# Six small edits to a convolution and spectral-mixing kernel: yeT's order, the conv band's set-up, the first load on two queues, halved last stores, Y's transposes behind the mixing's, and 15 junk matmuls

## Chip, cores, metric

One core of one Trainium2 chip. The metric is the device time of one execution in microseconds (us), the median of repeated runs. The time of the kernel before was 181.24 us (three runs, 180.69 to 181.25). Each execution also reports the span of the core's program, 1.8 us less than the time in the median, up to 3.1 us less in single executions; the profile's clock starts with the span. A transfer "lands" when its completion is signalled, here some 0.3 us after its last packet (177.89 against 177.55 us for the last store of the kernel before).

## The reference

Two layers in a row, cut to what matters:

```python
# x: (8, 3264, 192) float32; weight: (8 heads, 7 taps)
w = softmax(weight, axis=-1)
x[b, s, h, :] = sum_k w[h, k] * x_padded[b, s + k, h, :]     # causal conv, one filter per head
X = rfft(x, axis=1)[:, :64]                                   # 64 lowest modes
Y[b, m, :] = X[b, m, :] @ (w_r[m] + 1j * w_i[m])              # 64 complex 192 x 192 mixes
u = x + irfft(Y, n=3264)
out = u + relu(u @ w_ch)
```

## The kernel before

The program has three stages. Until about 66 us x is loaded by GpSimd (float32 cast to bf16 on the way), convolved by matmuls with a banded matrix, and brought to 64 modes. Until about 108 us the modes are mixed: 16 groups of weights, each loaded in two halves behind x on the same GpSimd queue. From there to the end the result is built in 108 units of two batches by one window of 122 positions, and stored.

The parts that the change touches (cuts marked):

```python
# start: softmax weights and one unit of x come by other queues than GpSimd's
nc.scalar.dma_start(out=wraw, in_=weight)                    # 224 bytes
nc.sync.dma_start(out=x32[:], in_=...)                       # 768 KB, x of batch 0, windows 10 to 17
load_unit(0, 2)                                              # first load of the GpSimd stream, 432 KB
...
# conv band: masks from an iota, then softmax, then 7 scaled masks summed by matmuls
nc.vector.tensor_copy(out=diagc[...], in_=diag[...])         # waits for GpSimd's iota
... softmax of wraw on VectorE and ScalarE ...
for k in range(KK):
    nc.vector.scalar_tensor_tensor(out=scaled[:, k, :, :], ...)
    for o in bps:                                            # the same sum into two banks
        nc.tensor.matmul(o[:, 0:H * NB], ident[:], scaled[:, k, :, :], ...)
for g in range(4):                                           # 4 copies: ScalarE takes bank 0, VectorE bank 1
    ...

# mixing: two groups g make 128 rows of Y (ymix), transposed into yeT
def mix_t(g, ymix):
    for t in range(2):
        nc.tensor.transpose(et[:, t, :], ymix[:, 64 * t:64 * t + P], ident[:])
    nc.vector.tensor_copy(out=yeT[:, :, P * (g // 2):P * (g // 2) + P], in_=et)

# 12 of the 16 groups go back from yeT to zy, two times 8 transposes
def y_back(half):
    for i in range(4):
        for e in range(2):
            nc.tensor.transpose(tp[...], yeT[:, e, 4 * half + i:n * B:B], ident[:])   # stride of 8
    nc.vector.tensor_copy(out=zy[...], in_=tp[...])

# the products with w_ch, first thing of the last stage
nc.tensor.matmul(o, yeT[:, e, b:2 * MODES * B:B], wn[:, :], ...)                      # stride of 8

for g in range(NGRP):
    m = mix(g)                                               # 12 matmuls, waits for the group's weights
    ... transposes of x (tp) that fill TensorE between the groups ...
        if g in (12, 13):
            y_back(g - 12)
    if m is not None:
        mix_t(g, m)
    ...

# last stage: one store per window and half of the batches, 384 KB, issued by SP
def finish_unit(u, zp):
    nc.vector.tensor_tensor(out=t[...], in0=zp[...], in1=x_all[...], op=ALU.add)
    if k == 0:
        return
    nc.sync.dma_start(out=dst, in_=t[r0:r1, :, :])
```

Of the kernel before, what the change touches and what calls it, by code (L numbers as in the profile page):

```python
# [9 lines left out]
ALU = mybir.AluOpType  # L10
ACT = mybir.ActivationFunctionType
AX = mybir.AxisListType
F32 = mybir.dt.float32
BF16 = mybir.dt.bfloat16
# [4 lines left out]
def kernel(  # L19
# [9 lines left out]
    nc = tc.nc  # L29
    B, S, D = x.shape  # L30
    H, KK = weight.shape
    MODES = moe_w_r.shape[0]
# [3 lines left out]
    P = 128  # L36
    WIN = 122
    OV = KK - 1
# [13 lines left out]
    constp = ctx.enter_context(tc.tile_pool(name="const", bufs=1))  # L52
# [20 lines left out]
    def load_last():  # L73
# [8 lines left out]
    ident = constp.tile([P, P], BF16, tag="ident")  # L82
# [10 lines left out]
    cband = cp1.tile([P, H, P], BF16, tag="cband")  # L93
# [3 lines left out]
    sp = setup_stack.enter_context(tc.tile_pool(name="setup", bufs=1))  # L97
    wraw = sp.tile([1, H, KK], F32, tag="wraw")
    nc.scalar.dma_start(out=wraw[:].rearrange("p h k -> p (h k)"),
                        in_=bass.AP(tensor=weight.tensor, offset=weight.offset, ap=[[H * KK, 1], [1, H * KK]]))  # L100

    x32 = sp.tile([P, 8, D], F32, tag="x32")
    nc.sync.dma_start(out=x32[:], in_=bass.AP(tensor=x.tensor, offset=x.offset + (WIN * 10 - OV) * D,
                                              ap=[[D, P], [WIN * D, 8], [1, D]]))
    load_unit(0, 2)
    diag = sp.tile([P, P], F32, tag="diag")
    nc.gpsimd.iota(diag[:], pattern=[[-1, P]], base=0, channel_multiplier=1,
# [33 lines left out]
    nc.vector.memset(ones[:], 1.0)  # L141
    nc.vector.memset(cband[:], 0.0)

    NB = 32 + OV
    diagc = sp.tile([P, NB], F32, tag="diagc")
    nc.vector.memset(diagc[0:32, 0:OV], -1.0)
    for g in range(4):
        i0 = OV if g == 0 else 0
        nc.vector.tensor_copy(out=diagc[32 * g:32 * g + 32, i0:NB],
                              in_=diag[32 * g:32 * g + 32, 32 * g - OV + i0:32 * g + 32])  # L150
    nc.vector.tensor_scalar(out=ident[:], in0=diag[:], scalar1=0.0, scalar2=None, op0=ALU.is_equal)

    halfpi = sp.tile([P, 1], F32, tag="halfpi")
    nc.vector.memset(halfpi[:], math.pi / 2)
    kprod = sp.tile([P, NWIN, MODES], F32, tag="kprod")
# [2 lines left out]
    def make_k(u):  # L158
# [20 lines left out]
    nc.vector.tensor_tensor(out=wrow[:], in0=wexp[:],  # L179
                            in1=wrec[:, :].unsqueeze(2).to_broadcast([1, H, KK]), op=ALU.mult)  # L180

    ps1 = ExitStack()
    pconv = ps1.enter_context(tc.tile_pool(name="pconv", bufs=3, space=PSUM))
    pxx = ps1.enter_context(tc.tile_pool(name="pxx", bufs=1, space=PSUM))
# [2 lines left out]
                     start=True, stop=True)  # L187
# [4 lines left out]

    scaled = sp.tile([P, KK, H, NB], BF16, tag="scaled")
    bps = [pxx.tile([P, 512], F32, tag=tag, name="bps") for tag in ("xt", "xp")]
    for k in range(KK):
        nc.vector.scalar_tensor_tensor(out=scaled[:, k, :, :],
                                       in0=diagc[:, :].unsqueeze(1).to_broadcast([P, H, NB]), scalar=float(k),
                                       in1=wsb[:, :, k:k + 1].to_broadcast([P, H, NB]),
                                       op0=ALU.is_equal, op1=ALU.mult)
        for o in bps:  # L200
            nc.tensor.matmul(o[:, 0:H * NB], ident[:], scaled[:, k, :, :].rearrange("p h i -> p (h i)"),  # L201
                             start=(k == 0), stop=(k == KK - 1))
    make_k(1)
    for g in range(4):
        i0 = OV if g == 0 else 0
        dst = cband[32 * g:32 * g + 32, :, 32 * g - OV + i0:32 * g + 32]
        srcv = bps[g % 2][32 * g:32 * g + 32, 0:H * NB].rearrange("p (h i) -> p h i", h=H)[:, :, i0:NB]
        if g % 2 == 0:
            nc.scalar.copy(out=dst, in_=srcv)
        else:  # L210
            nc.vector.tensor_copy(out=dst, in_=srcv)


    WFAC = -TWOPI * (1.0 - 4e-7) / S
# [26 lines left out]

    gst = constp.tile([P, GW], BF16, tag="gst")

    yeT = constp.tile([P, 2, 2 * MODES * B], BF16, tag="yeT")



# [152 lines left out]
    for p in range(4):  # L400
        k = 0
        for i in range(11):
            n = 8 if i < 4 else 7
# [75 lines left out]
    def y_back(half):  # L479
        tp = pt.tile([P, 1024], BF16, tag="p", name="yb")  # L480
        n = 16 * YPE
        for i in range(4):
            for e in range(2):
                c0 = D * i + 64 * e
                nc.tensor.transpose(tp[0:n, c0:c0 + P], yeT[:, e, 4 * half + i:n * B:B], ident[:])  # L485
        nc.vector.tensor_copy(out=zy[0:n, 4 * half:4 * half + 4, :],
                              in_=tp[0:n, 0:4 * D].rearrange("p (b e) -> p b e", b=4))

    def mix_t(g, ymix):
        zt = mixed[0]  # L490
        et = zt[:, 256:512].bitcast(BF16)[:, 0:2 * P].rearrange("p (t k) -> p t k", t=2)
        for t in range(2):
            nc.tensor.transpose(et[:, t, :], ymix[:, 64 * t:64 * t + P], ident[:])
        nc.vector.tensor_copy(out=yeT[:, :, P * (g // 2):P * (g // 2) + P], in_=et)



# [3 lines left out]
    zwps = []  # L501


    def zw_mm(h, k, banks):
        for i in range(2):
            b = 4 * h + 2 * k + i
            zp = banks[i % len(banks)]
            o = zp[:, D * i:D * i + D] if len(banks) == 1 else zp[:, 0:D]
            for e, wn in ((0, win0), (1, win1)):
                nc.tensor.matmul(o, yeT[:, e, b:2 * MODES * B:B], wn[:, :],  # L510
                                 start=(e == 0), stop=(e == 1), skip_group_check=True)
        zt = zwip.tile([P, 2 * D], BF16, tag=f"zw{h}{k}", name="zw")
        if len(banks) == 2:
            nc.vector.tensor_copy(out=zt[:, 0:D], in_=banks[0][:, 0:D])
            nc.scalar.copy(out=zt[:, D:2 * D], in_=banks[1][:, 0:D])
        else:
            nc.vector.tensor_copy(out=zt[:], in_=banks[0][:, 0:2 * D])
        b = 4 * h + 2 * k
        zwi[(h, 0, k)] = zt[:]
        zwi[(h, 1, k)] = zy[:, b:b + 2, :].rearrange("p b e -> p (b e)")  # L520
# [68 lines left out]
    def finish_unit(u, zp):  # L589
        h, w, k = u  # L590
        if k == 0:
            ts[h] = p3.tile([P, B // 2, D], F32, tag="t", name="t")
        t = ts[h]
        add = nc.vector.tensor_tensor(  # L594
            out=t[:, 2 * k:2 * k + 2, :],
            in0=zp[:, 0:2 * D].rearrange("p (i e) -> p i e", i=2),
            in1=x_all[:, 4 * h + 2 * k:4 * h + 2 * k + 2, w, :], op=ALU.add)
        if k == 0:
            return
        rows = ((0, 80), (80, LASTVALID)) if w == NWIN - 1 else ((0, P),)  # L600
        for r0, r1 in rows:
            dst = bass.AP(tensor=out.tensor, offset=out.offset + (4 * h * S + WIN * w + r0) * D,
                          ap=[[D, r1 - r0], [S * D, B // 2], [1, D]])
            nc.sync.dma_start(out=dst, in_=t[r0:r1, :, :])


    CH = 7
# [1 line left out]
    wq = [(0, worder[0]), (0, worder[1])]  # L609
# [9 lines left out]
    zps = []  # L619

    def bank(n):
        if n % 8 < 3:
            return pza.tile([P, 512], F32, tag="z", name="z")
        if n % 8 < 7:
            return pt.tile([P, 512], F32, tag="p", name="z")
        return py.tile([P, 512], F32, tag="y", name="z")

    def prefill():
        zps.append(bank(len(zps)))
        ab_full(seq[len(zps) - 1], zps[-1])  # L630

    def keep_warm(n):

        for _ in range(n):
            nc.tensor.matmul(zwps[0][:, 0:P], ident[:], ident[:], start=True, stop=True)

    for g in range(NGRP):
        last = g == NGRP - 1
        m = mix(g)
        if g == 6:  # L640
            wts0_stack.close()
            cTb = ctx.enter_context(tc.tile_pool(name="stashb", bufs=1)).tile([P, CTW], BF16, tag="cTb")
            nc.vector.memset(cTb[:, NSLOT * WIN:CTW], 0.0)
            cTs[3] = cTb[:, :]
        if g in (0, 1, 2):
            load_weights(g + 7, wp)
        elif 7 <= g and g + 4 < NGRP:
            load_weights(g + 4, None if g == 10 else wp)
        if not last:
            for _ in range(TPER[g]):  # L650
                t_next(2 if g < 6 else 3)
            if gq:
                g_part(gq.pop(0))
            if g == 2:
                load_weights(10, None)

            if g in (10, 11, 14):
                prefill()
            if g in (12, 13):
                y_back(g - 12)  # L660
        else:
            keep_warm(4)
        if m is not None:
            mix_t(g, m)
        if g == NGRP - 2:
            zwps += [pt.tile([P, 512], F32, tag="p", name="zwps") for _ in range(2)]
            prefill()
            prefill()
            keep_warm(6)
    zwps.append(py.tile([P, 512], F32, tag="y", name="zwps"))  # L670
    keep_warm(4)
    early_stack.close()

    padp = ctx.enter_context(tc.tile_pool(name="pad", bufs=1, side="right"))
# [10 lines left out]
    def gy(n):  # L685
        g_full(seq[n], zps[n], 1)
        finish_unit(seq[n], zps[n])
# [68 lines left out]
```

## Time and profile before

| | before |
|---|---|
| median time | 181.24 us |
| span of the profiled run | 178.87 us |
| last weights land, last mixing starts | 106.78, 107.26 us |
| first store issued, last add ends | 112.38, 174.41 us |
| last packet of the last store | 177.55 us |

An engine's digit in the page's slices is its busy share in tenths, and `PEclk` is the share of TensorE's full clock that was granted. The prediction below shows the rows for DMA and the chain of waits. Three more lines turn out to matter. From the page's queues (queue and kind: packets, MB, share of the 16 engines' span), the instruction queue of the kernel before:

```profile
q8 instruction: 16, 0.26, 0.6%
```

That is 16 packets of 16,384 bytes, each in flight for 0.9 to 1.5 us; by the name of the queue they are refills of an engine's instructions. From its issues, narrowed to the first load of GpSimd (KB, us from issue to landing):

```profile
x_all<-in_x_dram POOLq DMA_DIRECT2D x1, 432.0 KB, 6.6
```

And from SP's timeline (start, duration), one of the last stores being issued:

```profile
172.52 0.39 SPq L604 DMA_DIRECT2D out_dram<-t  x1
```

The first load, issued at 1.24 us, lands at 7.83; SP took 0.39 us to issue this store.

### The profile page before, as it was taken

How to read it: one execution, taken by the hardware profiler on the slowest of the kernel's cores; microseconds unless marked ns; L12 is line 12 of the kernel's file. 1: busy time of each engine (PE TensorE's matmuls, PEld its weight loads, DVE VectorE, ACT ScalarE, POOL GpSimd, SP SyncE). 2: the span in 40 equal slices, each digit the busy share in tenths (PEclk: the TensorE clock that was granted, in tenths of full speed). 3: DMA queues.
4: the chain of work that ended last, by engine and by line, in shares of the span. 5: the costliest groups of instructions: out<-in, count | busy, mean ns of one | idle time of the engine just before them, and what ended most of it. 6: DMA issues, size and time to landing. Idle time of an engine off the chain costs nothing.

```text
span 178.9 us, 5425 instructions
## 1 busy us (share of the span) xinstructions
PE 147.8 (83%) x2132; PEld 129.4 (72%) x2132; DVE 128.0 (72%) x260; ACT 112.6 (63%) x188; POOL 48.8 (27%) x74
## 2 busy tenths in 40 slices
PE   0472579888889979887786988999999999999970
PEld 0241459878779859886675876799999999999940
DVE  5879975552553546976767425699999999999990
ACT  2356973555557626775656214588888888888850
POOL 7998332549222344331544000000000000000000
PEclk9999558999999999999999799999999999999996
DMA  4999999999999999999999970669999999999996
GB/s 137 210 190 192 192 192 192 191 190 191 193 192 195 202 206 208 205 208 209 204 207 206 207 133 11 214 222 325 355 341 333 360 341 345 348 335 363 315 338 205
DMA packets 65813, 42.04 MB, mean 235 GB/s; under 512 B 29212, under 2 KB 65788, under 8 KB 65788
## 3 DMA queue, kind: packets, MB, share of 16 engines
q0 software_dynamic: 36048, 19.75, 79.4%
q1 hardware_dynamic: 29738, 21.96, 37.0%
q8 instruction: 16, 0.26, 0.6%
q14 instruction: 9, 0.07, 0.1%
q10 hardware_dynamic: 2, 0.00, 0.0%
HBM read 40.28 MB, written 21.01 MB: 343 GB/s over the span
## 4 chain that ended last, share of the span: by engine, by line
PE 63%; DVE 16%; DMA 11%; issue 4%; POOL 1%; ACT 1%; DVEq 0%; POOLq 0%; ACTq 0%
PE z L542 19%; PE z L559 14%; PE xp L290 8%; PE cp L268 8%; DMA wt<-in_moe_w_r_dram 6%; DMA wt<-in_moe_w_i_dram 5%; DVE x_all L277 5%; PE tp L426 4%; PE yp L463 2%; PE bps L201 2%; PE yb L485 2%; PE tp L302 1%; DVE kprod L223 1%; PE z L524 1%; DVE xs L294 1%
## 5 line engine op out<-in xcount | busy, mean ns | idle before, releaser
L594 DVE TENSOR_TENSOR t<-z,x_all 128x384 f32<-128x384 f32 x108 | 59.6, 557 | 3.3 <-PE z L559 1.7
L564 ACT ACTIVATE z<-z 128x384 f32<-128x384 f32 x108 | 50.9, 475 | 12.0 <-PE z L542 1.4
L542 PE MATMUL z<-zw,gst 64*128 64x384 bf16 x204 | 46.4, 323 | 0.0
L559 PE MATMUL z<-zy,gst 64*128 64x384 bf16 x204 | 46.1, 323 | 0.2
L542 PE MATMUL z<-win,cTa 64*128 64x192 bf16 x375 | 41.1, 243 | 0.0
L275 ACT CAST x_all<-cp 122x864 bf16<-122x864 f32 (+2 forms) x34 | 28.6, 878 | 16.3 <-PE cp L268 16.2
L542 PEld LDWEIGHTS <-cTa 64*128 64x128 bf16 x450 | 35.1, 94 | 2.7
L268 PE MATMUL cp<-x_all,cband 128*128 128x192 bf16 (+2 forms) x192 | 24.8, 276 | 9.2 <-DVE x_all L277 3.9
L268 PEld LDWEIGHTS <-cband 128*128 128x128 bf16 x192 | 18.7, 105 | 13.0 <-issue 5.7
L277 DVE CAST x_all<-cp 122x768 bf16<-122x768 f32 (+2 forms) x14 | 14.7, 1055 | 14.1 <-PE cp L268 13.7
L61 POOL DMA_DIRECT2D x_all<-in_x_dram x23 | 22.0, 973 | 8.0 <-DMA x_all<-in_x_dram 6.9
L290 PE MATMUL xp<-x_all,fst 122*128 122x192 bf16 (+1 forms) x216 | 22.0, 251 | 0.9 <-DVE x_all L277 0.5
L431 ACT COPY cTa<-tp 128x854 bf16<-128x854 bf16 (+1 forms) x16 | 14.0, 911 | 10.5 <-PE tp L426 10.4
L290 PEld LDWEIGHTS <-fst 122*128 122x128 bf16 (+1 forms) x216 | 18.2, 99 | 2.1 <-DVE x_all L277 0.7
L542 PEld LDWEIGHTS <-gst 64*128 64x128 bf16 x204 | 19.1, 94 | 0.6 <-issue 0.6
L542 PE MATMUL z<-win,cTb 64*128 64x192 bf16 x135 | 19.2, 243 | 0.0
L542 PE MATMUL z<-wB,cTa 64*128 64x192 bf16 x75 | 18.2, 243 | 0.0
L559 PEld LDWEIGHTS <-gst 64*128 64x128 bf16 x204 | 16.1, 93 | 1.0 <-POOLq L576 0.9
L542 PEld LDWEIGHTS <-cTb 64*128 64x128 bf16 x162 | 14.4, 94 | 1.1
L430 DVE COPY cTa<-tp 128x854 bf16<-128x854 bf16 (+1 forms) x17 | 10.6, 623 | 5.7 <-PE tp L426 5.2
L426 PE MATMUL tp<-ident,x_all 122*128 122x122 bf16 x216 | 13.6, 217 | 0.0
L259 POOL DMA_DIRECT2D wt<-in_moe_w_r_dram x14 | 8.6, 613 | 18.1 <-DMA x_all<-in_x_dram 5.6
(105 smaller groups left out, 173.6 us busy)
## 6 DMA issues: line engine op xcount, KB each, us to landing
out_dram<-t SPq DMA_DIRECT2D x52, 384.0 KB, 3.9
wt<-in_moe_w_r_dram POOLq DMA_DIRECT2D x14, 288.0 KB, 11.5
wt<-in_moe_w_i_dram POOLq DMA_DIRECT2D x14, 288.0 KB, 11.4
x_all<-in_x_dram POOLq DMA_DIRECT2D x8, 432.0 KB, 12.2
x_all<-in_x_dram POOLq DMA_DIRECT2D x7, 480.0 KB, 11.9
x_all<-in_x_dram POOLq DMA_DIRECT2D x8, 384.0 KB, 13.8
x<-in_x_dram SPq DMA_DIRECT2D x1, 768.0 KB, 5.0
fst<-in_moe_w_r_dram POOLq DMA_DIRECT2D x2, 288.0 KB, 10.0
```

Source lines behind the costliest of these rows:

```text
L61: nc.gpsimd.dma_start(out=x_all[:, b, c0:c0 + n, :], in_=src)
L268: nc.tensor.matmul(cp[:, j, 0:GRP * n].rearrange("p (w e) -> p w e", w=n), cband[:, h, :], x_all[:, b, w0:w0 + n, GRP * h:GRP * h + GRP], ...
L275: nc.scalar.copy(out=dst, in_=srcv)
L277: nc.vector.tensor_copy(out=dst, in_=srcv)
L290: nc.tensor.matmul(xp[:, 0:D], fst[0:k, c, :], x_all[0:k, b, c, :], start=(u == FIRST[b] and c == w0), stop=(u == LAST[b] and c == w0 + n ...
L426: nc.tensor.transpose(tp[:, WIN * k:WIN * k + WIN], slot_lhsT(p, k0 + k), ident[0:WIN, 0:WIN])
L430: nc.vector.tensor_copy(out=got[0][0], in_=got[0][1])
L431: nc.scalar.copy(out=got[1][0], in_=got[1][1])
L542: return nc.tensor.matmul(o, lhsT, rhs, start=start, stop=stop, skip_group_check=True, tile_position=(lo, 0))
L559: return [lambda: nc.tensor.matmul(zp[:, 0:2 * D], gst[lo:hi, WIN * w:WIN * w + P], zwi[(h, 1, k)][lo:hi, :], start=False, stop=(r == 1), ...
L564: return nc.scalar.activation(out=zp[:, 0:2 * D], in_=zp[:, 0:2 * D], func=ACT.Relu)
L594: add = nc.vector.tensor_tensor(out=t[:, 2 * k:2 * k + 2, :], in0=zp[:, 0:2 * D].rearrange("p (i e) -> p i e", i=2), in1=x_all[:, 4 * h + ...
```

## The change

It means to shorten three stretches: the start (band ready earlier, first unit of x sooner), the end of the mixing (yeT laid out so that weight loads read it without a stride, the mixing's transposes ahead of Y's, 15 junk matmuls meant to keep TensorE's clock up), and the last stores. A junk matmul is one whose result nobody reads: `keep_warm(o, n)` multiplies the identity by itself n times into the bank o. The kernel before has 14 of them elsewhere already.

```diff
-    nc.sync.dma_start(out=x32[:], in_=...)
+    for q, eng in enumerate((nc.sync, nc.scalar)):
+        eng.dma_start(out=x32[:, 4 * q:4 * q + 4, :], in_=...)
...  (masks diagc and ident are built after the softmax instead of before)
-        for o in bps:
-            nc.tensor.matmul(o[:, 0:H * NB], ident[:], scaled[:, k, :, :]..., 
+        for half, o in enumerate(bps):
+            nc.tensor.matmul(o[:, 0:H // 2 * NB], ident[:], scaled[:, k, 4 * half:4 * half + 4, :]...,
...  (the band copies: 4 per engine, each of half the heads)
-    yeT = constp.tile([P, 2, 2 * MODES * B], BF16, tag="yeT")
+    yeT = constp.tile([P, 2, B, 2 * MODES], BF16, tag="yeT")
-        nc.vector.tensor_copy(out=yeT[:, :, P * (g // 2):P * (g // 2) + P], in_=et)
+        q = 16 * (g // 2)
+        nc.vector.tensor_copy(out=yeT[:, :, :, q:q + 16], in_=et.rearrange("p t (q b) -> p t b q", b=B))
...  (readers of yeT lose the stride: yeT[:, e, b, :])
-        if k == 0:
+        split = (h, w) in wq[-2:]
+        if k == 0 and not split:
             return
...  (the last two windows are stored in halves of 192 KB)
-            if g in (12, 13):
-                y_back(g - 12)
+            if g == 11:
+                junk = bank(2)
         if m is not None:
             mix_t(g, m)
+        if g in (12, 13):
+            y_back(g - 12)
+        if g in (11, 12, 13):
+            keep_warm(junk, 5)
```

More of the change, by code (lines that the diff above doesn't have):

```diff
@@ L102 @@
     x32 = sp.tile([P, 8, D], F32, tag="x32")
-    nc.sync.dma_start(out=x32[:], in_=bass.AP(tensor=x.tensor, offset=x.offset + (WIN * 10 - OV) * D,
-                                              ap=[[D, P], [WIN * D, 8], [1, D]]))
+    for q, eng in enumerate((nc.sync, nc.scalar)):
+        eng.dma_start(out=x32[:, 4 * q:4 * q + 4, :],
+                      in_=bass.AP(tensor=x.tensor, offset=x.offset + (WIN * (10 + 4 * q) - OV) * D,
+                                  ap=[[D, P], [WIN * D, 4], [1, D]]))
     load_unit(0, 2)
@@ L142 @@
     nc.vector.memset(cband[:], 0.0)
-    NB = 32 + OV
-    diagc = sp.tile([P, NB], F32, tag="diagc")
-    nc.vector.memset(diagc[0:32, 0:OV], -1.0)
-    for g in range(4):
-        i0 = OV if g == 0 else 0
-        nc.vector.tensor_copy(out=diagc[32 * g:32 * g + 32, i0:NB],
-                              in_=diag[32 * g:32 * g + 32, 32 * g - OV + i0:32 * g + 32])
-    nc.vector.tensor_scalar(out=ident[:], in0=diag[:], scalar1=0.0, scalar2=None, op0=ALU.is_equal)
     halfpi = sp.tile([P, 1], F32, tag="halfpi")
@@ L180 @@
                             in1=wrec[:, :].unsqueeze(2).to_broadcast([1, H, KK]), op=ALU.mult)
+    NB = 32 + OV
+    diagc = sp.tile([P, NB], F32, tag="diagc")
+    nc.vector.memset(diagc[0:32, 0:OV], -1.0)
+    for g in range(4):
+        i0 = OV if g == 0 else 0
+        nc.vector.tensor_copy(out=diagc[32 * g:32 * g + 32, i0:NB],
+                              in_=diag[32 * g:32 * g + 32, 32 * g - OV + i0:32 * g + 32])
+    nc.vector.tensor_scalar(out=ident[:], in0=diag[:], scalar1=0.0, scalar2=None, op0=ALU.is_equal)
     ps1 = ExitStack()
@@ L199 @@
                                        op0=ALU.is_equal, op1=ALU.mult)
-        for o in bps:
-            nc.tensor.matmul(o[:, 0:H * NB], ident[:], scaled[:, k, :, :].rearrange("p h i -> p (h i)"),
+        for half, o in enumerate(bps):
+            nc.tensor.matmul(o[:, 0:H // 2 * NB], ident[:],
+                             scaled[:, k, 4 * half:4 * half + 4, :].rearrange("p h i -> p (h i)"),
                              start=(k == 0), stop=(k == KK - 1))
@@ L205 @@
         i0 = OV if g == 0 else 0
-        dst = cband[32 * g:32 * g + 32, :, 32 * g - OV + i0:32 * g + 32]
-        srcv = bps[g % 2][32 * g:32 * g + 32, 0:H * NB].rearrange("p (h i) -> p h i", h=H)[:, :, i0:NB]
-        if g % 2 == 0:
-            nc.scalar.copy(out=dst, in_=srcv)
-        else:
-            nc.vector.tensor_copy(out=dst, in_=srcv)
+        for half, o in enumerate(bps):
+            dst = cband[32 * g:32 * g + 32, 4 * half:4 * half + 4, 32 * g - OV + i0:32 * g + 32]
+            srcv = o[32 * g:32 * g + 32, 0:H // 2 * NB].rearrange("p (h i) -> p h i", h=H // 2)[:, :, i0:NB]
+            if half == 0:
+                nc.scalar.copy(out=dst, in_=srcv)
+            else:
+                nc.vector.tensor_copy(out=dst, in_=srcv)
     WFAC = -TWOPI * (1.0 - 4e-7) / S
@@ L484, in y_back @@
                 c0 = D * i + 64 * e
-                nc.tensor.transpose(tp[0:n, c0:c0 + P], yeT[:, e, 4 * half + i:n * B:B], ident[:])
+                nc.tensor.transpose(tp[0:n, c0:c0 + P], yeT[:, e, 4 * half + i, 0:n], ident[:])
         nc.vector.tensor_copy(out=zy[0:n, 4 * half:4 * half + 4, :],
@@ L493, in mix_t @@
             nc.tensor.transpose(et[:, t, :], ymix[:, 64 * t:64 * t + P], ident[:])
-        nc.vector.tensor_copy(out=yeT[:, :, P * (g // 2):P * (g // 2) + P], in_=et)
+        q = 16 * (g // 2)
+        nc.vector.tensor_copy(out=yeT[:, :, :, q:q + 16],
+                              in_=et.rearrange("p t (q b) -> p t b q", b=B))
     zwi = {}
@@ L509, in zw_mm @@
             for e, wn in ((0, win0), (1, win1)):
-                nc.tensor.matmul(o, yeT[:, e, b:2 * MODES * B:B], wn[:, :],
+                nc.tensor.matmul(o, yeT[:, e, b, :], wn[:, :],
                                  start=(e == 0), stop=(e == 1), skip_group_check=True)
@@ L597, in finish_unit @@
             in1=x_all[:, 4 * h + 2 * k:4 * h + 2 * k + 2, w, :], op=ALU.add)
-        if k == 0:
+        split = (h, w) in wq[-2:]
+        if k == 0 and not split:
             return
+        i0 = 2 * k if split else 0
+        nb = 2 if split else B // 2
         rows = ((0, 80), (80, LASTVALID)) if w == NWIN - 1 else ((0, P),)
         for r0, r1 in rows:
-            dst = bass.AP(tensor=out.tensor, offset=out.offset + (4 * h * S + WIN * w + r0) * D,
-                          ap=[[D, r1 - r0], [S * D, B // 2], [1, D]])
-            nc.sync.dma_start(out=dst, in_=t[r0:r1, :, :])
+            dst = bass.AP(tensor=out.tensor, offset=out.offset + ((4 * h + i0) * S + WIN * w + r0) * D,
+                          ap=[[D, r1 - r0], [S * D, nb], [1, D]])
+            nc.sync.dma_start(out=dst, in_=t[r0:r1, i0:i0 + nb, :])
     CH = 7
@@ L628, in prefill, with keep_warm @@
     def prefill():
-        zps.append(bank(len(zps)))
+        zps.append(junk if len(zps) == 2 else bank(len(zps)))
         ab_full(seq[len(zps) - 1], zps[-1])
-    def keep_warm(n):
+    def keep_warm(o, n):
         for _ in range(n):
-            nc.tensor.matmul(zwps[0][:, 0:P], ident[:], ident[:], start=True, stop=True)
+            nc.tensor.matmul(o[:, 0:P], ident[:], ident[:], start=True, stop=True)
     for g in range(NGRP):
@@ L658 @@
                 prefill()
-            if g in (12, 13):
-                y_back(g - 12)
+            if g == 11:
+                junk = bank(2)
         else:
-            keep_warm(4)
+            keep_warm(zwps[0], 4)
         if m is not None:
             mix_t(g, m)
+        if g in (12, 13):
+            y_back(g - 12)
+        if g in (11, 12, 13):
+            keep_warm(junk, 5)
         if g == NGRP - 2:
@@ L668 @@
             prefill()
-            keep_warm(6)
+            keep_warm(zwps[0], 6)
     zwps.append(py.tile([P, 512], F32, tag="y", name="zwps"))
-    keep_warm(4)
+    keep_warm(zwps[0], 4)
     early_stack.close()
```

## The prediction

> **What bounds the kernel now.** I read the page's slices first, then DMA and clock in short stretches, then the chain of waits, then the time from issue to landing of single transfers. The page's last three slice rows of part 2:
>
> ```profile
> PEclk9999558999999999999999799999999999999996
> DMA  4999999999999999999999970669999999999996
> GB/s 137 210 190 192 192 192 192 191 190 191 193 192 195 202 206 208 205 208 209 204 207 206 207 133 11 214 222 325 355 341 333 360 341 345 348 335 363 315 338 205
> ```
>
> The DMA row is 9 from the second slice (4.5 us) to the 23rd (about 103 us), then falls to 0 at about 107 us. So until then one stream, x and then the weights, never pauses. Table of stretches (columns: stretch, busy time of each engine, granted clock, DMA share, GB/s; the DMA share counts overlapping packets and can exceed 1):
>
> ```profile
> 4.50:5.00 0.50, 0.00 (x0) 0.00 (x0) 0.42 (x4) 0.01 (x1) 0.50 (x2) 1.00 1.16 334
> 5.00:5.50 0.50, 0.00 (x0) 0.00 (x0) 0.20 (x1) 0.24 (x1) 0.50 (x2) 1.00 1.58 204
> ...
> 100.25:100.50 0.25, 0.25 (x4) 0.25 (x3) 0.12 (x1) 0.23 (x1) 0.00 (x0) 0.53 1.20 203
> ...
> 105.75:106.00 0.25, 0.25 (x9) 0.17 (x3) 0.00 (x0) 0.00 (x0) 0.00 (x0) 1.00 0.58 123
> 106.00:106.25 0.25, 0.25 (x5) 0.25 (x4) 0.00 (x0) 0.00 (x0) 0.00 (x0) 1.00 0.13 25
> ```
>
> The reader is to see the stream settle by 5.0 us, run at a share of 1.6 while x comes and 1.2 while weights come, and dry up at 106. Single transfers: the two halves of the 13th weight group land at 96.7 and 98.1 us, of the 14th at 99.5 and 100.9, the 15th at 102.4 and 103.8, the 16th at 105.3 and 106.76 (issued 96.66, 10.1 us to landing). That is 2.84 us per group. The chain of waits, in order of time, from there to the last stage:
>
> ```profile
> 98.24 0.48 PE yp L463 x11
> 98.72 0.85 PE tp L426 x14
> 99.58 1.46 PE yb L485 x8
> 101.03 0.67 PE yp L463 x12
> 101.70 1.54 PE tp L426 x14
> 103.24 1.36 PE yb L485 x8
> 104.59 0.02 issue
> 104.62 0.14 DVE zy L486
> 104.75 0.34 issue
> 105.09 0.29 DVE yeT L494
> 105.38 0.04 issue
> 105.42 0.48 PE yp L463 x12
> 105.90 1.10 PE z L532 x12
> 107.00 0.33 PE zwps L635 x6
> 107.33 0.43 PE yp L463 x12
> ```
>
> So the last mixing starts at 107.3 us, only about 0.5 us after its weights landed at 106.76. Behind it come ymix, two transposes, the copy to yeT and the zw products, and from 113 us to 172 us the last stage, where matmuls (0.57 us per unit in the chain), VectorE adds (557 ns each) and stores (about 345 GB/s) all run nearly full. No line of that stage changes except its last stores.
>
> [...] the clock is halved from 100.25 to about 103.6 us, 3.4 us, right after a stretch (96.8 to 100.25) of idle and mostly transposes. [...] the strided 128x128 loads of yeT take 145 ns at full clock, those of cTa 98 ns. [...]
>
> **The change part by part.**
>
> Start (x32 on two queues, softmax ahead of the band masks, band by halves of heads). The 14 band matmuls go from 304 to 152 columns. They occupy 3.72 us in the chain (7.19 to 10.91), 266 ns each; halved they are 133 ns, 14 x 133 = 1.9 us, so VectorE's seven scaled operations (2.79 us, 6.66 to 9.45) become the pace. The band is done about 10.91 - (9.45 + 0.27) = 1.2 us earlier. VectorE no longer idles 0.82 us for the iota, and can cover the 0.3 us waits for the exponential and the broadcast: up to 0.5 us more. The eight half-size band copies cost about what four did (0.96 us a side). So the band is some 1.5 us earlier. All of it lies beside the DMA stream: x lands when it lands, and weights behind it. On the end: **0**. The only way from here to the end is the stream's own start. Between 1.5 and 3.0 us the DMA moves only 28 to 94 GB/s, so two shorter issues could let x32 flow up to 0.4 us earlier, and everything queued behind it. I give that four chances in ten: **-0.15 us**.
>
> Mixing's end (Y's transposes behind the mixing's, junk matmuls, yeT by batches). Before, VectorE's yeT copy of the 14th group waited behind eight yb transposes, which ran at half clock with strided loads, 1.36 us. Now the order is tp, mixing transposes, yb, five junk matmuls. Walk: the 14th mixing still waits for weights of 100.93, starts at 101.05, ends at 101.5; 14 tp 0.85 us at full clock, 102.35; transposes 0.28, 102.65; the yeT copy ends at 103.1. The 15th mixing then waits for weights (103.8) and starts at 103.9, not 105.42. With yb (8 x 0.08 = 0.65) and junk (0.35) TensorE is free by then. 15th mixing 0.48, two prefills 1.10, six warm matmuls 0.33: ready for the last at 105.9. But its weights land at 106.76. It starts about 0.1 us later, 106.85 against 107.26: **-0.40 us**. If the clock still halves, the walk ends at about 106.6, still before the weights. The reorder saves 1.4 us on TensorE, of which the stream lets 0.4 through.
>
> Behind the last mixing: the yeT copy now reads PSUM with a stride of eight elements. [...] +0.13 us, to about 425 ns [...]. The first four zw products stand at 0.56 us (140 ns each, the strided load); contiguous they should cost what the later four cost in the chain, 0.33 us plus the first load: -0.18 us. Net **-0.05 us**.
>
> Stores of the last two windows by halves: the last four adds end at 172.94, 173.45, 173.94 and 174.42; the last store is issued at 174.44 and lands at 177.94. A half moves in 0.52 us against 1.04 at 370 GB/s. But from 172.5 to 176.5 us the DMA stands at 356 to 373 GB/s without a hole: four tiles in 4 us. Early halves only queue behind what is moving. **-0.10 us** (between 0 and 0.4).
>
> Sum: -0.15 - 0.40 - 0.05 - 0.10 = -0.7 us, so 181.24 - 0.7 = 180.5 us.
>
> **Rivals.** (a) The mixing's end is bound by TensorE, not by the last landing: then the full 1.4 us and some of the start come through, 179.2 us. For it speaks the chain, which names yb on 2.8 us; against it the landing at 106.76. (b) The stream starts earlier than I think and all of it moves up by 0.5 to 1 us: 179.5 to 180. The slow ramp before 3.0 us speaks for it; [...]. (c) The strided yeT copy costs much more than 0.13 us, or junk matmuls delay the 15th mixing: then it takes the place of the wait removed and the time stays at 181.2. Little speaks for it, as there are 0.9 us of slack ahead of the last landing. (d) The store tail is latency-bound: halves save half a transfer, 0.5 us, 180.1. The full DMA rate after 172.5 us speaks against it.
>
> **Range and chances.** Before, three runs spread over 0.56 us. Rivals (a), (b) and (d) pull down, (c) up: 179.4 to 181.2 holds it 8 times in 10. Over 2% faster needs 177.6 us, more than (a), (b) and (d) sum to: 0.03. Over 2% slower: 0.01.
>
> **What would show it.** Right: the band's first use near 10.4 us instead of 12; the 16th weight group still landing at 106.4 to 106.8 us; TensorE idle about 0.9 us just ahead of the last mixing, released by that DMA; yeT copies near 0.42 us; yeT loads near 95 to 100 ns; the last stage as long as before. Wrong: a last landing over 0.5 us earlier (the start reaches the end after all), a last mixing that waits for anything but its weights, or a DMA hole after 172.5 us that the halves fill.

## The result, and the profile after

The changed kernel took 182.07 us (median of 4 runs, 181.72 to 182.39) against 180.97 us for the kernel before (4 runs, 180.64 to 181.25). The ratio is 1.0061, with a 95% interval of 1.0032 to 1.0091: slower by 0.6%. A ratio is the mean time of one kernel's fast runs over that of the other's in the same rounds, so it is not quite the ratio of the medians quoted. All runs of the study were in the fast state.

The page of the changed kernel, its rows for clock and DMA:

```profile
PEclk9999999999999999999999999999999999999997
DMA  5999999999999999999999950769999998999994
GB/s 151 192 190 192 192 192 192 191 190 194 190 193 193 205 207 207 207 207 208 204 208 205 207 99 16 259 217 339 341 348 344 345 346 287 369 348 357 305 336 159
```

TensorE's clock was not halved in this run while it had work, which the reader sees in the first row (all slices at 9 but the last); and the stream still ends in the 24th slice. Its chain of waits at the end of the mixing (some pieces of under 0.05 us cut at the dots):

```profile
97.57 9.88 DMA wt<-in_moe_w_i_dram
107.45 0.04 issue
107.49 0.51 PE yp L467 x12
...
108.08 0.34 ACT ymix L476
108.42 0.05 issue
108.47 0.30 PE yp L497 x2
...
108.86 0.43 DVE yeT L499
109.30 0.05 issue
109.34 0.52 PE zwps L516 x4
```

The transposes of Y have left the chain: the last mixing starts 0.04 us after its weights. But the weights land at 107.45 instead of 106.78. The copy to yeT takes 0.43 us instead of 0.30, the first four products 0.52 instead of 0.56. The last stage then starts 0.3 us later than before (first store 112.70 against 112.38), and this comes through whole: from the first store issued to the last add it is 62.03 us in both.

The rest of the loss is at the other end. DMA in stretches of half a microsecond; the columns are as in the prediction's table. First the kernel before, then the changed one:

```profile
176.50:177.00 0.50, 0.00 (x0) 0.00 (x0) 0.00 (x0) 0.00 (x0) 0.00 (x0) 0.50 0.70 235
177.00:177.50 0.50, 0.00 (x0) 0.00 (x0) 0.00 (x0) 0.00 (x0) 0.00 (x0) 0.50 0.09 31
```

```profile
177.50:178.00 0.50, 0.00 (x0) 0.00 (x0) 0.00 (x0) 0.00 (x0) 0.00 (x0) 1.00 0.49 161
178.00:178.50 0.50, 0.00 (x0) 0.00 (x0) 0.00 (x0) 0.00 (x0) 0.00 (x0) 0.69 0.07 23
```

From the end of the last add to the last packet of a store it was 3.14 us before (174.41 to 177.55) and is 4.00 us now (174.73 to 178.73). From there to the end of the span it was 1.32 us and is 1.60 us. So the 1.47 us between the two spans are 0.32 of start, 0.86 of tail and 0.28 behind it. The lines that answer to the three shown of before are, from the queues, the issues and SP's timeline of the changed kernel:

```profile
q8 instruction: 17, 0.28, 0.6%
```

```profile
x_all<-in_x_dram POOLq DMA_DIRECT2D x1, 432.0 KB, 7.7
```

```profile
172.85 1.06 SPq L613 DMA_DIRECT2D out_dram<-t  x1
```

There is one instruction packet more; it starts at 172.2 us and takes 1.25 us. Right behind it, SP took 1.06 us to issue a store. And GpSimd's first load lands 1.1 us later (8.90 us against 7.83). These three lines gave the theories for the experiments:

- **F**: the 15 junk matmuls make TensorE's program 30 instructions longer (each matmul comes with a weight load: the pages count 2147 of each against 2132), so that one more 16 KB refill falls into the last stores and holds up one of the DMA engines. The stretches above fit that: at full pace the 16 engines' share is 1.10 (from 174.5 to 176.5 us before), and the 0.07 from 178.0 to 178.5 us is what one engine alone makes of it (1.10 / 16).
- **S**: the halved stores themselves hold SP up.
- **Q**: the second queue at the start delays GpSimd's stream, and so the last weights.
- **D**: the rival to F and S: all of the loss comes from the later weights.

### The profile page after: what moved, and what is told of

Its sections match the earlier page's. It is cut to its first block, busy times and chain, and to the rows that moved or that the text cites. A ratio compares the mean times of both kernels' runs of the same rounds, so it can differ in the third digit from the quotient of the medians.

```text
span 180.3 us, 5464 instructions
## 1 busy us (share of the span) xinstructions
PE 147.1 (82%) x2147; PEld 128.3 (71%) x2147; DVE 129.5 (72%) x262; ACT 113.2 (63%) x190; POOL 48.7 (27%) x74
## 4 chain that ended last, share of the span: by engine, by line
DMA 53%; PE 36%; POOL 3%; issue 2%; DVE 1%; ACT 1%; DVEq 0%; POOLq 0%; ACTq 0%
DMA x_all<-in_x_dram 30%; DMA wt<-in_moe_w_i_dram 23%; PE z L548 19%; PE z L565 13%; POOL x_all L61 3%; PE z L530 1%; PE yp L467 1%; DVE t L600 1%; POOL wt L263 1%; PE zwps L516 1%; PE tp L430 1%; ACT z L570 0%; DVEq L764 0%; DVE yeT L499 0%; ACT ymix L476 0%
## 5 line engine op out<-in xcount | busy, mean ns | idle before, releaser
L272 PE MATMUL cp<-x_all,cband 128*128 128x192 bf16 (+2 forms) x192 | 26.6, 293 | 8.7 <-DVE x_all L324 5.3
L272 PEld LDWEIGHTS <-cband 128*128 128x128 bf16 x192 | 19.9, 111 | 12.8 <-DVE x_all L324 6.5
L467 PEld LDWEIGHTS <-xt 128*32 128x32 bf16 x192 | 5.3, 147 | 12.0 <-issue 6.2
(106 smaller groups left out, 178.5 us busy)
```

The lines of the kernel that those rows point to most:

```text
L272: nc.tensor.matmul(cp[:, j, 0:GRP * n].rearrange("p (w e) -> p w e", w=n), cband[:, h, :], x_all[:, b, w0:w0 + n, GRP * h:GRP * h + GRP], ...
```

## The experiments

Each kernel ran six times (a profiled run and five rounds), beside eleven runs of the kernel before on the same chip. "Mean span" below is the mean over executions, each reported to 0.1 us; those of the kernel before scatter with a standard deviation of 0.25 to 0.4 us (0.76 beside fin_early), so a difference of means has a standard error of 0.1 to 0.4 us. "Tail" is the time from the end of the last add to the last packet of a store in the profiled run, worked out from the trace's records.

| kernel | ratio (95%) | mean span against before | refills in the trace (last at) | tail |
|---|---|---|---|---|
| before | | | 16 (166.0) | 3.14 |
| changed | 1.0061 (1.0032 to 1.0091) | not taken | 17 (172.2) | 4.00 |
| a_nosplit | 1.0096 (1.0063 to 1.0130) | +1.73 | 17 (172.2) | 3.93 |
| a_nojunk | 1.0027 (0.9997 to 1.0057) | +0.43 | 16 (166.3) | 2.86 |
| a_oneq | 1.0068 (1.0031 to 1.0105) | +1.30 | 17 (172.8) | 4.03 |
| b_split | 1.0015 (0.9989 to 1.0040) | +0.17 | 17 (179.9) | 2.94 |
| b_extra15 | 1.0033 (1.0008 to 1.0058) | +0.82 | 17 (172.3) | 3.94 |
| b_extra48 | 1.0013 (0.9991 to 1.0035) | +0.49 | 17 (170.9) | 3.69 |
| best | 1.0008 (0.9987 to 1.0030) | +0.30 | 16 (165.6) | 2.77 |
| best_oldyet | 0.9995 (0.9973 to 1.0017) | +0.07 | 16 (165.8) | 2.87 |
| b_twoq | 1.0004 (0.9964 to 1.0044) | +0.31 | 16 (166.1) | 2.91 |
| b_reorder | 0.9994 (0.9955 to 1.0032) | -0.11 | 16 (165.5) | 3.22 |
| b_band | 0.9991 (0.9953 to 1.0030) | -0.08 | 16 (166.7) | 2.79 |
| b_reorder_split | 1.0024 (0.9976 to 1.0073) | +0.49 | 17 (180.5) | 3.12 |
| b_two_sp | 1.0010 (0.9973 to 1.0046) | +0.29 | 16 (165.3) | 3.15 |
| b_twoq_early | 0.9967 (0.9938 to 0.9997) | -0.31 | 17 (179.5) | 2.89 |
| fin_oldyet | 0.9977 (0.9946 to 1.0008) | -0.31 | 16 (165.8) | 2.90 |
| fin_yet | 1.0007 (0.9970 to 1.0044) | +0.35 | 16 (167.1) | 2.93 |
| fin_early | 1.0011 (0.9956 to 1.0067) | -0.03 | 17 (179.6) | 2.99 |

### The store tail: halves or instructions?

**a_nosplit**, the changed kernel with whole stores:

```diff
-        split = (h, w) in wq[-2:]
+        split = False
```

> The changed kernel with its last stores whole again (everything else of the change kept). Theory S (SP's issue of the halves and the extra instruction fetch near the end hold the stores up; 1.46 us between the two profiled spans, of which 0.33 us lie before the last stage and 0.85 us or more in the store tail): about 0.7 to 1.0 us faster than the changed kernel, so 181.1 to 181.4 us. Theory F (the extra 16 KB instruction fetch at 172.2 us alone does it, whatever the stores' size): the fetch is still there, so at most 0.3 us faster than the changed kernel. Rival D (the whole loss comes from the weights landing later): no difference, 182.0.

It was not faster (1.0096). The refill is still there at 172.2 us, and the tail stays at 3.93 us. So the halves are not what costs. S falls as the main cause. That it was slower still than the changed kernel (1.0061, in another session) is not explained; its profiled execution, at a span of 180.0, was among its fastest.

**a_nojunk**, the changed kernel without its junk matmuls:

```diff
-        if g in (11, 12, 13):
-            keep_warm(junk, 5)
```

> The changed kernel without its 15 junk matmuls (30 TensorE instructions less, as many as before). Theory F: the instruction fetch near 172 us is gone and the store tail is as before although the halves stay, 0.7 to 1.0 us faster than the changed kernel, about 181.2. Theory S (halves): at most 0.2 us faster. If the junk matmuls are what keeps the clock up, the half clock returns near 100 us; the last mixing should still start with its weights, since some 0.9 us of slack is there.

Its ratio is 1.0027, an interval that includes no change; its mean span lies 0.43 us over the kernel before and some 0.8 us under the changed kernel (mean span 179.35; the changed kernel's four executions had 180.3, 180.2, 180.5 and 179.8, in another session). The 17th refill is gone, no issue of SP from 172 us on takes more than 0.60 us, and the tail is 2.86 us although the halves stay. This is what F expected.

**b_extra15** puts the same 30 instructions into the kernel before, where TensorE idles, and nothing else (the first convolution starts at 12.75 us instead of 12.04; b_band below shows that the start has slack):

```diff
     nc.tensor.matmul(wps[:, 0, 0:H * KK], ones[:], wrow[...], start=True, stop=True)
+    for _ in range(15):
+        nc.tensor.matmul(wps[:, 1, 0:H * KK], ones[:], wrow[...], start=True, stop=True)
```

> The kernel before with 15 idle matmuls (30 TensorE instructions) added near 6 us, where TensorE waits for VectorE; nothing else. Theory F (an extra 16 KB fetch of TensorE's instructions falls into the last stores because the program is 30 instructions longer): a 17th fetch near 172 us, an issue of a store by SP of about 1 us near 172.9 instead of 0.39, and about 0.8 to 1.0 us slower than before. Rival J (the junk matmuls cost time where they stand, behind the mixing's transposes): no change, within 0.2 us of before.

The instruction queue in this trace, then the DMA of the tail in stretches of 1 us, of the kernel before and of b_extra15, then SP's issue behind the refill:

```profile
q8 instruction: 17, 0.28, 0.6%
```

```profile
176.00:177.00 1.00, 0.00 (x0) 0.00 (x0) 0.00 (x0) 0.00 (x0) 0.00 (x0) 0.50 0.90 304
177.00:178.00 1.00, 0.00 (x0) 0.00 (x0) 0.00 (x0) 0.00 (x0) 0.00 (x0) 0.50 0.05 16
```

```profile
176.00:177.00 1.00, 0.00 (x0) 0.00 (x0) 0.00 (x0) 0.00 (x0) 0.00 (x0) 0.81 0.81 273
177.00:178.00 1.00, 0.00 (x0) 0.00 (x0) 0.00 (x0) 0.00 (x0) 0.00 (x0) 0.50 0.11 36
```

```profile
173.37 0.52 SPq L607 DMA_DIRECT2D out_dram<-t  x1
```

The 17th refill came at 172.3 us, the tail grew from 3.14 to 3.94 us, and the kernel was slower by 0.33%, an interval that leaves out no change (0.60 us in mean time, 0.82 in mean span). So the cost comes without the junk matmuls' place, and the rival J, by which they cost through the time that they take where they stand, falls: ahead of the last mixing TensorE idles 1.00 us with them and 1.03 us without (a_nojunk). So does D as the only cause: the weights are not late here (107.07 us), and the kernel is slower all the same. Two expectations missed: SP's issue took 0.52 us here, not 1 us, and the loss was below the 0.8 us named. The tail grew all the same, so the long issue is not needed for it. Over all traces the five with a refill between 170.9 and 172.8 us have tails of 3.69 to 4.03 us, the other fourteen 2.77 to 3.22.

**b_extra48**, the same with `range(48)`:

> The same with 48 idle matmuls (96 instructions), some 2.7 us of idle TensorE time filled near 6 to 9 us. Theory F: the 17th fetch moves 66 instructions earlier, at about 35 instructions per us to some 170.3 us; it still falls in the store tail, so slower than before by 0.4 to 1.0 us. Rival (it is the count, not the place, of fetches): exactly as the run with 15.

The refill moved to 170.9 us (expected: some 170.3), and the tail was 3.69 us. The loss was 0.49 us in mean span, and the ratio, 1.0013, does not tell it from none, so between F and the count alone this run does not decide. It fits the reading that the earlier the refill, the more of its delay is made up before the end. So does the 16th refill, at 162 to 167 us, which every kernel has and which leaves no long tail by itself. A 17th that comes after the last packets, as in b_split (179.9 us), cost the stores nothing (tail 2.94 us).

**b_split**, the kernel before with halved last stores alone (the diff's last-stores part):

> The kernel before with only its last two windows' stores split into halves. Theory S: 0.5 to 0.9 us slower than before, with SP issues of the halves at 0.45 us or more. Theory F: no instruction fetch near 172 us, so the same as before within 0.2 us or up to 0.4 us faster, as the change intended.

The tail in the trace was 2.94 against 3.14 us, and yet the kernel was not faster (1.0015). Part of the gain is chance: over the traces without a refill in the last stores, the tail is 2.77 to 3.12 us with halves (five, mean 2.91) and 2.79 to 3.22 us with whole stores (nine, mean 2.99). What the halves cost lies behind it. At the end of the program SP waits for its store semaphores one after another, 0.06 us from one to the next where nothing holds it. Before, six of these waits are over by 175.2 us, and after the last landing at 177.89 only two are left. With the halves the third in the list is held until 177.59 us, and the rest follows: the tenth and last ends at 178.02. So data that is there 0.35 us sooner (last packet 177.20 against 177.55) ends at the same span, 178.89 against 178.87 us. From the last packet to the end of the span it is 1.6 to 1.7 us in all seven traces with halves, and 1.2 to 1.3 us in all twelve with whole stores.

### The start: what delays the stream?

**a_oneq**, the changed kernel with the first unit on one queue:

```diff
-    for q, eng in enumerate((nc.sync, nc.scalar)):
-        eng.dma_start(out=x32[:, 4 * q:4 * q + 4, :], ...
+    nc.sync.dma_start(out=x32[:], ...
```

> The changed kernel with the first x unit on one queue again. Theory Q (the second queue makes the slowest DMA engine's stream end later: last weights packet 107.13 against 106.43 us): last packet near 106.4 again and 0.3 to 0.7 us faster than the changed kernel. Rival (which engines the instruction fetches fall on sets the last landing): no systematic change, within 0.2 us.

First load and last weights landed earlier in its trace (7.78 and 107.14 us), as Q expects, but the time did not follow (1.0068). The profiled execution was one of two slow ones (spans 181.2 and 181.1, the other four 179.4 to 180.2), and its chain shows why. Ahead of the last mixing TensorE waits for the weights; then the clock is halved just when the first products come:

```profile
109.03 1.46 PE zwps L514 x8
```

In the changed kernel's trace the same eight took 0.83 us. This run decides nothing on Q, but suggests a risk that the prediction had not seen: TensorE freed early only idles longer, and the clock may be halved behind it. That the idling halves it is not shown: of the ten traces with about 1.0 us of idling there, two have the halved clock behind it (this one and fin_yet).

**b_twoq**, the kernel before with the two queues alone:

> The kernel before with only its first x unit loaded on two queues. Theory Q (the slowest DMA engine starts the GpSimd stream about 1 us late and stays late): first GpSimd load lands at 8.8 us or later instead of 7.8 to 8.5, the last weights at 107.4 to 107.6 instead of 106.75 to 107.16, and the whole 0.2 to 0.4 us slower than before, since the last mixing follows the landing. Rival (the spread of landings is chance): landings inside the one-queue range, time within 0.1 us.

First load at 8.92 us, last weights at 107.63, mean span +0.31 us: the landings are where Q puts them. The timed ratio does not show it (1.0004, an interval that reaches from -0.4 to +0.4%).

**b_two_sp** and **b_twoq_early** ask what about it delays the stream. The first issues both halves from SP. The second keeps the two queues, but issues the small weight load behind the second half instead of ahead of it, so that both halves go out at 0.74 us (in the changed kernel the second goes at 1.28):

```diff
# b_two_sp
-    for q, eng in enumerate((nc.sync, nc.scalar)):
+    for q, eng in enumerate((nc.sync, nc.sync)):
# b_twoq_early
-    nc.scalar.dma_start(out=wraw[...], in_=weight)      # ahead of x32
     ... x32 on sync and scalar ...
+    nc.scalar.dma_start(out=wraw[...], in_=weight)      # behind x32
```

> The kernel before with x32 loaded in two pieces, both issued by SP. If the second queue is what delays the GpSimd stream: first GpSimd load lands at 7.7 to 8.5 us as with one piece, time as before within 0.1 us. If cutting in two does it: lands at 8.8 us or later, 0.2 to 0.3 us slower.

> The kernel before with x32 on two queues, the ACT half issued at 0.74 us ahead of the small weight load instead of at 1.28 us behind it. If the late start of the second half delays the GpSimd stream: first GpSimd load lands before 8.5 us, time as before. If two queues as such do it: at 8.8 us or later again, 0.2 to 0.3 us slower than before; softmax starts later, which nothing waits for.

GpSimd's first load, in the traces of b_twoq and of b_twoq_early:

```profile
x_all<-in_x_dram POOLq DMA_DIRECT2D x1, 432.0 KB, 7.7
```

```profile
x_all<-in_x_dram POOLq DMA_DIRECT2D x1, 432.0 KB, 6.8
```

Cutting in two on one queue leaves the landing alone (8.01 us; its mean span of +0.29 has two executions at 180.1 and 179.7 beside four at 178.4 to 178.9, so that number decides nothing). Two queues with both halves issued at once leave it alone too (8.05 us, last weights 107.08), and this kernel was the only one faster than before outside its interval (0.9967); among 17 kernels one such interval can be chance, and fin_early below did not confirm it. So it is not the second queue as such that delays the stream. Nor is it a late second half as such: in b_two_sp the second half was issued 0.50 us behind the first (1.24 us) without any delay. What is left is both together: a second half on ScalarE's queue, behind the small load there. Over all traces: SP's queue alone or both halves at once, 15 traces, first load at a median of 8.01 us and last weights at 107.07; second half late on ScalarE's queue, 4 traces, 8.91 and 107.54. One trace of the 15 (b_band) had 9.36 and 108.01, so a late stream also happens by itself. Why it delays the stream is open: the records do not name the engine of a packet.

### The end of the mixing and the order of yeT

**b_reorder**, the kernel before with `y_back` behind `mix_t`, and nothing else:

> The kernel before with only Y's transposes moved behind the mixing's (no junk matmuls, old order of yeT). The prediction's step: the last mixing starts within 0.1 us of the landing of its weights instead of 0.48 us after, 0.3 to 0.4 us faster. Rival (b_split's trace had the last mixing right at the landing in the old order too, because there the landing was 0.3 us later): gain only 0 to 0.2 us on average.

The last mixing started 0.04 us after its weights (106.95 after 106.91), as predicted. The gain was 0.11 us in mean span, not 0.4, as the rival said. The traces show why. Eight have the old order. In six of them the last mixing starts 0.04 us after its weights as well, TensorE having been free for 0.33 to 0.43 us (in b_two_sp at 106.44, with a landing as early as 106.77). Only two show the wait: the one that the prediction rests on (0.48 us), the only one of the eight in which the clock was halved from 100.27 to 103.7 us, and b_extra48 (0.45 us), whose first convolution started 2.3 us late. Over the eight that is 0.11 us to be saved on average. In the new order the halved clock of one trace did no harm: b_reorder_split's was halved from 100.45 us, and TensorE was free at 106.64, 0.19 us ahead of the mixing.

**best** and **best_oldyet**: the changed kernel with one queue and without junk matmuls, with the new and with the old order of yeT:

```diff
# best: changed kernel, minus the second queue, minus keep_warm(junk, 5)
# best_oldyet: the same, with
-    yeT = constp.tile([P, 2, B, 2 * MODES], BF16, tag="yeT")
+    yeT = constp.tile([P, 2, 2 * MODES * B], BF16, tag="yeT")
```

> The changed kernel without the junk matmuls and with the first x unit on one queue. Theory Q + F: 16 fetches, the first GpSimd load lands near 7.8 us instead of 8.9, the last weights near 106.8 to 107.1; then -0.4 us for the mixing's end, +0.1 for the slower copy to yeT, -0.2 for the halves: 0.3 to 0.6 us faster than before, and 0.4 us faster than the changed kernel without the junk alone (181.1).

> As the one before it, but yeT in the old interleaved order, so that the copy takes 0.29 us again and the weight loads of yeT 0.145 us. If the new order is a loss behind the last mixing (0.13 us more for the copy, 0.04 us less for the first products, as the changed kernel's trace reads): 0.1 us faster than the one before it, 180.2 to 180.4. If the strided loads delay the mixing's end instead: slower by 0.1 to 0.5 us.

Neither beat the kernel before. The landings were as expected, the time was not: best was expected 0.3 to 0.6 us under before and lies at +0.30 in mean span. The old order was the better by 0.24 us in mean span (standard error 0.17, so not resolved), against 0.09 that the two traces' durations give (copy 0.424 against 0.292, first products 0.52 against 0.57).

**b_band**, the band set-up alone:

> The kernel before with only the start's band set-up of the change (softmax ahead of the masks, halves of the heads). The first convolution starts about 2 us earlier (9.8 instead of 11.9 us), and the time is the same within 0.15 us, because the weights land when the stream brings them. Rival (an earlier front lets loads be issued earlier): last landing before 106.6 us and 0.2 us or more faster.

No change (0.9991). The profiled execution happened to have a late stream (first load 9.36 us) and was the second slowest of its six. That the band is ready 2 us earlier is worth nothing, as the prediction said.

### Sums of the parts

**b_reorder_split**, the reordering and the halves in the kernel before:

> The kernel before with Y's transposes behind the mixing's and the last stores by halves, nothing else: the two parts of the change that no run speaks against, in 4266 TensorE instructions. Sum of -0.1 to -0.4 us and -0.2 us: 180.2 to 180.5, 0.2 to 0.6 us faster than before. If single-run spans misled me and the halves bring nothing in timed runs either, the same as before within 0.1 us.

A miss: 1.0024, and +0.49 us, with two executions at 180.3 and 179.9 beside four from 178.8 to 179.2. The halves bring nothing in timed runs.

**fin_oldyet** and **fin_yet** keep only the band and the reordering, with the old and the new order of yeT:

> Of the change only the band set-up and the reordering of Y's transposes: spans 0.1 to 0.2 us under before (b_reorder gave -0.11, b_band -0.08 in mean span), the fastest of all kernels here; ratio 0.998 to 1.000.

> The same with the new order of yeT. If the slower copy (0.424 against 0.292 us) lies on the path behind the last mixing and the faster loads give only 0.04 back: 0.1 us slower than the one before it, up to 0.25 as the earlier pair of runs read. If the order is neutral: the same within 0.05 us in mean span.

fin_oldyet was a little better than expected (0.9977, -0.31 us), its interval just including no change. fin_yet ran in two groups: four executions at 178.5 to 178.8 us and two, the profiled one among them, at 179.8 and 180.3. The profiled one has the halved clock behind the last mixing again:

```profile
109.04 1.17 PE zwps L514 x8
```

The four alone are 0.2 us above fin_oldyet's six (178.3 to 178.6), which would be the cost of the new order once more; but they were picked after the fact, and all six are 0.67 us above.

**fin_early** adds the two queues with both halves at once:

> Of the change the band set-up, the reordering and the two queues, the latter with both halves issued ahead of the small weight load; old order of yeT, no junk matmuls, whole stores. b_twoq_early and fin_oldyet each gave -0.31 us in mean span. If they add: -0.5 to -0.6 us, ratio 0.996 to 0.997. If both removed the same wait behind the landing of the last weights: -0.3 us, ratio 0.998.

They did not add: 1.0011, spans from 178.1 to 180.0 us. No mix of the parts beats the kernel before by more than the scatter of the runs; most have a lower ratio than the changed kernel.

## Why the prediction was wrong

It said 180.5 us, in 179.4 to 181.2; measured were 182.07. Its frame held: the stream of loads bounds everything to 107 us, and a part that moves neither the stream nor the tail was worth nothing (b_band: -0.08 us in mean span, ratio 0.9991). The terms of its sum did not.

- **The junk matmuls, counted only as time in TensorE's slack.** This is the largest failure: the walk adds their 0.35 us where they stand and finds slack, which is right, and leaves out that they are instructions. The traces show the instructions coming over a DMA queue (q8, 16 packets of 16,384 bytes before, 17 in the changed kernel): with 30 instructions more the 17th refill came at 172.2 to 172.3 us and the tail grew by 0.8 us (a_nosplit, b_extra15), which is 0.33% of the time in b_extra15. That the refill holds up one DMA engine, on which a sixteenth of the last stores waits, is the reading that fits: in after, a_nosplit, a_oneq and b_extra15 about one engine's pace of packets is left in flight for the last 0.8 to 0.9 us, in the traces without such a refill for 0 to 0.5 us. The records do not name the engine.
- **Start, "-0.15 us".** The step that "two shorter issues could let x32 flow up to 0.4 us earlier, and everything queued behind it" failed. The first half lands earlier (4.46 us), the second when the whole did (5.64 against 5.76), and the first load of the stream behind it lands 1.1 us later (8.90 against 7.83). b_twoq puts the term at about +0.3 us in span, not resolved in its ratio. The band's part, "**0**", was right (b_band); the band came even earlier than worked out, 9.76 us for the first convolution against the 10.4 named.
- **Mixing's end, "-0.40 us".** The mechanism was right: the last mixing follows its weights by 0.04 us in all eleven traces with the new order, and where the clock was halved TensorE was free at 106.64, the 106.6 of the walk. The size was off because the 0.48 us of waiting was read from one trace, with a halved clock, and taken for the kernel's rule; in six of eight traces of the old order there is nothing to save. b_reorder measured -0.11 us, within the scatter. Rival (a), a bound on TensorE, is refuted. The prediction's "idle about 0.9 us just ahead of the last mixing" came true (1.0 us); whether it raises the risk of a halved clock behind it, which was not named, is not shown.
- **Behind the last mixing, "-0.05 us".** The copy's 425 ns, +0.13 us on the measured 292, was the author's estimate, for which the trace of the kernel before has no figure; it was met (424). The loads' 95 to 100 ns were met too (97, from 145). But the four products took 0.52 us, not 0.38. The prediction had read 0.56 us as "140 ns each"; the trace has 140 ns from the first to the second and 83 ns from each to the next, in the old order as in the new. Only the first gap shrank, to 92 ns. In place of -0.18 stands -0.04, and the term turns to +0.09 in the traces; the timed pair (+0.24) does not resolve it.
- **Stores, "-0.10 us".** That the halves "only queue behind what is moving" fits the tails, 2.91 against 2.99 us in the mean. What failed is the unspoken step from there to the end: behind the last packet come 1.6 to 1.7 us with halves against 1.2 to 1.3, because the waits for the stores stand in a fixed order. b_split measured +0.17 us, which its interval does not tell from 0.

Added up as an estimate from the single-part runs, in mean span: +0.82 (refill) +0.31 (two queues) +0.24 (yeT) +0.17 (halves) -0.11 (order) -0.08 (band) = +1.35 us. In mean time, in which the result is given, the same runs sum to 0.60 + 0.12 + 0.24 + 0.25 - 0.06 - 0.11 = +1.04 us, where 182.07 - 180.97 = 1.10 us was measured. With an error of 0.1 to 0.3 us on each, the sum fits, which is no proof of its terms: only the first is significant by itself, so some 0.6 us of the loss are shown, and how the rest divides is open.

## What to carry to other kernels

Where DMA bounds the last stage, count instructions as well as time: here a refill was a DMA of 16,384 bytes, and 30 idle instructions brought one at 172.3 us, among the last stores, where the tail went from 3.14 to 3.94 us (b_extra15). Ask of a gain that frees an engine early what it waits for next, and how much that wait varies from run to run, before a single trace's slack is booked as a gain: here it came with a halved clock that seven of the eight traces in the old order did not have at that place. And when several small edits are bundled, measure each one alone: here one edit of "no cost" outweighed all the others.
